# x^T of rows 512 to 2047: one transposing transfer for each block of 512 rows in place of five

## The chip, the cores and the metric

The kernel runs on one core of one Trainium2 chip. The metric is the device time of one execution in microseconds (us). Before the change the median of three runs is 182.51 us (182.13 to 182.59).

## The reference

Two linear-attention blocks A and B run over the same x (2048 rows, 640 columns, bf16), and a gate computed from x mixes their outputs row by row. For each block, with 32 heads of width 20:

```python
qkv = (x @ wqkv).reshape(B, S, 3, H, Dh)          # q, k, v by head
phi = lambda t: jnp.where(t > 0, t + 1, jnp.exp(t)) + 1e-6
pq, pk = phi(q), phi(k)
kv = jnp.einsum("bhsd,bhse->bhde", pk, v)
z = jnp.einsum("bhsd->bhd", pk)
num = jnp.einsum("bhqd,bhde->bhqe", pq, kv)
den = jnp.einsum("bhqd,bhd->bhq", pq, z)[..., None] + 1e-6
o = num / den                                     # then back to (S, D), @ wo
g = _sigmoid((x * gate_w).sum(-1, keepdims=True))
return g * a + (1 - g) * b                        # a, b: the two blocks' outputs
```

## The kernel before

Every projection on TensorE (PE) needs x with its 640 columns on the partitions, so the kernel holds a tile `xT` of 128 partitions x 5 x 2048: for each of the five groups c of 128 columns (a "column block"), the 2048 rows of x along the free axis. The rows are counted in blocks n of 512 (`HB`) and in chunks i of 128; block 1 is chunks 4 to 7, block 2 chunks 8 to 11, block 3 chunks 12 to 15.

Block 0 is not transposed by a transfer: its rows are loaded as they stand into `xn` and turned by PE (line 293), with VectorE (DVE) copying the result into `xT` (line 296). Blocks 1 to 3 come into `xT` straight from memory by transposing transfers, issued by SyncE (SP) at line 220: for each block five of them, one for each column block, 15 in all. The weights of k and q of block A are `wkA` and `wqA`; they are loaded from lines 203 and 217 ahead of the transposing transfers, on the same SP queue. Behind the transposing transfers SP issues the rows of blocks 1 to 3 once more, untransposed, into `xn` (line 1317), then v's weights `wvA` (1235) and the output weights `woA` (1242, 1245). All of SP's transfers are issued in the order of the code; each raises one of eight semaphores in turn (`DMAHW0` to `DMAHW7` in the listings below), and a transfer waits for the one that had the same semaphore before it.

The order on PE, DVE and ScalarE (ACT) is written out by hand in the string `FIRST`: each name is one step, and each engine executes what the steps give it in that order. The ones that matter here:

- `D4` to `D15` are the k projection of chunk 4 to 15 (`KFirst`, matmuls in `k_mm`, line 338). `D4` is cut into its five column blocks, `D4.c0` to `D4.c4`, with other work set between them:

```python
U0.n0 D2.top D4.c0 D4.c1 E.p1s E.P2 D4.c2 D4.c3 D3.clamp D3.lift0 tq3 sq03 U0.exp0 U0.lift0 tq1 D3.top D3.gl
sq01 D4.c4 E.exp0 tq2 D4.exp0 U0.n1 D4.gl sq02 ...
```

- `U0.n0` and `U0.n1` are a part of the q projection for block 0 and block 1 (line 393); `E.P1` and `E.P2` are q for block 0 alone (line 753).
- `sq03`, `sq01` and their like are sums and differences of two row blocks of `xT`, made by DVE (line 426) into `SQ` for the fast (Strassen-like) q product (line 527); `sq03` takes column blocks 0 and 1 of block 1, `sq01` column blocks 0 to 3.
- `D9` is the first step on block 2, `D15` the first on block 3.

Each reader of `xT` waits for the transfers that wrote what it reads. Where several readers on one engine follow one another, the first one carries the wait.

Of the kernel before, what the change touches and what calls it, by code (L numbers as in the profile page):

```python
# [9 lines left out]
P = 128  # L10
# [7 lines left out]
DT = D // P  # L18
# [3 lines left out]
HB = 512  # L22
# [56 lines left out]
def kernel(  # L79
# [11 lines left out]
    nc = tc.nc  # L91
    x2 = A_x.flatten_outer_dims()
# [43 lines left out]
    xT = persist.tile([P, DT, S], BF16, name="xT")  # L136
# [79 lines left out]
    for lo, hi in ((0, 2), (2, 4), (4, DT)):  # L216
        nc.sync.dma_start(out=wq[0][:, lo:hi, :], in_=wq_dram[0][:, lo:hi, 0:D])
    for n in range(1, NB):
        for c in range(DT):
            nc.sync.dma_start_transpose(  # L220
                out=xT[:, c, n * HB:(n + 1) * HB], in_=x2[n * HB:(n + 1) * HB, c * P:(c + 1) * P]
            )


    make_identity(nc, ident[:])
    for r in range(4):
# [3 lines left out]
        out=spread[:].rearrange("p (h t) -> p h t", t=TW), in_=I4[:, :, None].to_broadcast([P, H, TW])  # L230
    )
    for lo in range(0, HF, K6):
        part = maskE[:, lo:min(lo + K6, HF)]
        for sign, base in ((1, 0), (-1, Dh - 1)):
            nc.gpsimd.affine_select(
                out=part, in_=part, pattern=[[-sign * Dh, part.shape[1] // Dh], [0, Dh]],
# [3 lines left out]
    for rows, n in ((slice(0, 2 * H), H // 2), (slice(2 * H, P), H)):  # L240
        nc.gpsimd.tensor_copy(
            out=E4_rows[rows, 0:n], in_=I4[rows, 0:n, None].to_broadcast([rows.stop - rows.start, n, Dh])
# [1071 lines left out]
    with tc.manual_schedule():  # L1314
        pts = k_first()
        for n in range(1, NB):
            nc.sync.dma_start(
                out=xn[:, n * CB:(n + 1) * CB, :], in_=x2[n * HB:(n + 1) * HB, :].rearrange("(q p) d -> p q d", p=P)
# [325 lines left out]
```

## Time and profile before

| what | value |
|---|---|
| median of three runs | 182.51 us |
| the profiled execution's own time | 182.31 us |
| its span, from the first to the last instruction | 180.5 us |
| PE weight loads busy | 117.6 us |
| transposing transfers | 15, all on SP's queue |

The profile gives the busy time of each engine, a chain of waits followed back from the last instruction, the waits of each engine by releaser, and a timeline whose rows merge neighbouring instructions of one kind. "PEld" is PE's weight load, which runs beside the matmuls. For a transfer the trace has its time on the issuing queue ("SPq") and the time from the start of its issue to its landing, when the last of its data is there and its semaphore is complete. A busy PE is not PE at its peak, since the ends of matmuls are modelled.

### The profile page before, as it was taken

The page shows a single profiled execution, that of the slowest core. Times are in us where ns is not written, and L with a number is a line of the kernel's source. Part 1 is how long each engine was busy: PE and PEld are TensorE (multiplying, and loading weights), DVE is VectorE, ACT ScalarE, POOL GpSimd, SP SyncE. Part 2 cuts the span into 40 slices and gives each one's busy share as a digit, 9 for nine tenths or more (in the row PEclk, how much of TensorE's full clock was granted, in tenths as well). Part 3 has the DMA queues.
Part 4 walks back from the last instruction along what each step waited for, and adds up shares of the span by engine and source line. Part 5 has one row for each costly group of instructions (what it writes and reads, how often), then busy time and mean ns, then how long its engine had stood idle before and what let it go on. Part 6 is the DMA issues. An engine that isn't in the chain of part 4 may idle for free.

```text
span 180.5 us, 3397 instructions
## 1 busy us (share of the span) xinstructions
PE 176.9 (98%) x1276; PEld 117.6 (65%) x1276; DVE 152.0 (84%) x287; ACT 112.0 (62%) x235; POOL 4.4 (2%) x19
## 2 busy tenths in 40 slices
PE   8999999999999999999999999999999999999993
PEld 3666666665666677666656676766678777777772
DVE  1479999999999996888899997987988988686774
ACT  2098988999763434587778686774815756456410
POOL 7100000000000000000000000000000000000000
PEclk9999999999999999999999999999999999999999
DMA  5995449976035015000000024144901560133123
GB/s 184 284 187 91 97 106 291 356 158 182 0 112 185 8 54 181 2 0 0 2 4 2 0 32 153 31 127 123 264 3 48 167 153 0 40 137 119 73 101 120
DMA packets 21602, 18.85 MB, mean 104 GB/s; under 512 B 9298, under 2 KB 21074, under 8 KB 21586
## 3 DMA queue, kind: packets, MB, share of 16 engines
q1 hardware_dynamic: 20722, 17.82, 35.3%
q10 hardware_dynamic: 864, 0.82, 1.3%
q8 instruction: 10, 0.16, 0.4%
q14 instruction: 6, 0.05, 0.1%
HBM read 11.86 MB, written 4.80 MB: 92 GB/s over the span
## 4 chain that ended last, share of the span: by engine, by line
PE 96%; ACT 2%; DVE 1%; issue 0%
PE q L527 16%; PE kA L338 11%; PE kB L338 9%; PE gs L845 9%; PE gs L1333 9%; PE oy L1129 6%; PE oz L1129 5%; PE ox L1129 5%; PE ow L1129 4%; PE kB L527 3%; PE qA L393 3%; PE gB L815 2%; PE gA L815 2%; PE warm L252 2%; ACT e L551 1%; PE q L393 1%
## 5 line engine op out<-in xcount | busy, mean ns | idle before, releaser
L338 PEld LDWEIGHTS <-xT 128*128 128x128 bf16 x280 | 27.3, 98 | 15.1 <-DVE xT L296 0.2
L338 PE MATMUL kA<-wkA,xT 128*128 128x320 bf16 (+1 forms) x160 | 24.8, 304 | 0.0
L551 ACT ACTIVATE e<-q 128x512 bf16<-128x512 f32 x32 | 18.5, 599 | 5.7 <-PE q L527 5.2
L557 DVE TENSOR_SCALAR e<-e 128x640 bf16<-128x640 bf16 (+2 forms) x59 | 19.0, 334 | 2.9 <-ACT e L551 2.6
L338 PE MATMUL kB<-wkB,xT 128*128 128x320 bf16 x120 | 19.2, 299 | 0.0
L551 ACT ACTIVATE e<-kB 128x640 bf16<-128x640 f32 (+1 forms) x18 | 11.4, 647 | 7.3 <-PE kB L527 3.2
L551 ACT ACTIVATE e<-kA 128x640 bf16<-128x640 f32 x16 | 11.4, 720 | 5.8 <-PE kA L338 5.2
L533 DVE TENSOR_TENSOR q<-q,p 128x512 f32<-128x512 f32 x16 | 11.1, 695 | 1.7 <-PE q L527 1.2
L564 DVE SCALAR_TENSOR_TENSOR pk<-kB,e 128x640 bf16<-128x640 f32 (+1 forms) x16 | 11.6, 735 | 0.4
L1129 PEld LDWEIGHTS <-xT 128*128 128x128 bf16 x85 | 8.1, 98 | 2.9
L1129 PEld LDWEIGHTS <-pqTA 128*128 128x128 bf16 x85 | 8.1, 98 | 2.8
L1192 ACT COPY u<-ox 128x320 f32<-128x320 f32 x8 | 3.4, 425 | 10.4 <-PE ox L1129 10.4
L1129 PEld LDWEIGHTS <-pqTB 128*128 128x128 bf16 x80 | 7.8, 98 | 3.0
L527 PE MATMUL q<-xT,wqB 128*128 128x512 bf16 x32 | 9.7, 379 | 0.0
L1134 DVE TENSOR_TENSOR osb<-oz,u 128x320 bf16<-128x320 f32 (+2 forms) x18 | 7.9, 452 | 1.9 <-PE oz L1129 1.6
L527 PE MATMUL q<-SQ,TM 128*128 128x512 bf16 x32 | 8.5, 379 | 0.0
L1333 PEld LDWEIGHTS <-xn 128*128 128x128 bf16 x64 | 6.1, 98 | 3.1 <-issue 0.7
L815 PEld LDWEIGHTS <-xn 128*128 128x128 bf16 x64 | 6.3, 98 | 2.8
L845 PEld LDWEIGHTS <-xn 128*128 128x128 bf16 x64 | 6.1, 98 | 2.9 <-issue 0.7
L564 DVE SCALAR_TENSOR_TENSOR pk<-kA,e 128x640 bf16<-128x640 f32 x8 | 6.5, 818 | 0.4 <-DVE e L557 0.2
L564 DVE SCALAR_TENSOR_TENSOR pqTB<-q,e 128x512 bf16<-128x512 f32 x10 | 6.7, 682 | 0.0
L1129 PE MATMUL oz<-MB,xT 128*128 128x320 bf16 (+2 forms) x45 | 6.8, 284 | 0.0
(205 smaller groups left out, 376.3 us busy)
## 6 DMA issues: line engine op xcount, KB each, us to landing
out_dram<-osb SPq DMA_DIRECT2D x14, 160.0 KB, 1.8
xn<-in_A_x_dram SPq DMA_DIRECT2D x3, 640.0 KB, 5.8
wvA<-in_A_wqkv_dram SPq DMA_DIRECT2D x1, 800.0 KB, 9.1
wkB<-in_B_wqkv_dram SPq DMA_DIRECT2D x1, 800.0 KB, 4.5
wqB<-in_B_wqkv_dram SPq DMA_DIRECT2D x1, 800.0 KB, 7.1
wvB<-in_B_wqkv_dram SPq DMA_DIRECT2D x1, 800.0 KB
MA<-m_rows SPq DMA_DIRECT2D x1, 800.0 KB, 5.1
MB<-m_rows SPq DMA_DIRECT2D x2, 400.0 KB, 4.1
```

The costliest lines, as they stand in the source:

```text
L338: nc.tensor.matmul(pt[:, hf, 0:n], lhsT=xT[:, c, i * P:(i + 1) * P], rhs=wk[b][:, c, hf * HF:hf * HF + n], start=(c == 0), stop=(c == DT - 1),
L393: nc.tensor.matmul(dst, lhsT=mixed(wq[b][:, c, :], m), rhs=xT[:, c, n * HB:(n + 1) * HB], start=first, stop=last,)
L527: nc.tensor.matmul(dst, lhsT=left(c), rhs=right(c), start=first and k == 0, stop=last and k == len(cs) - 1, skip_group_check=not first,)
L533: nc.vector.tensor_tensor(out=dst, in0=acc, in1=sb, op=ALU.add)
L551: nc.scalar.activation(out=self.part(self.e, k), in_=self.srcs[k](), func=ACT.Exp)
L557: nc.vector.tensor_scalar(self.e, self.e, 1.0, EPS, op0=ALU.min, op1=ALU.add)
L564: nc.vector.scalar_tensor_tensor(out=self.part(self.dst, k), in0=src(), scalar=1.0 + EPS, in1=self.part(self.e, k), op0=ALU.add, op1=ALU.max,)
L815: nc.tensor.matmul(pt[:, hf, 0:HF], lhsT=xn[:, i, c * P:(c + 1) * P], rhs=pk[:, i, hf * HF:(hf + 1) * HF], start=(i == 0), stop=(i == ST - 1),
L845: nc.tensor.matmul(pt[:, n, 0:HF], lhsT=left[:, i, n * P:(n + 1) * P], rhs=right[:, i, :], start=(first and i == 0), stop=(i == hc - 1), s ...
L1129: nc.tensor.matmul(dst, lhsT=left[:, c, r0:r0 + P], rhs=right[:, c, :], start=(first and c == 0), stop=(c == DT - 1), skip_group_check=not ...
L1134: nc.vector.tensor_tensor(out=dst, in0=acc, in1=sb, op=ALU.add)
L1333: nc.tensor.matmul(dst[n], lhsT=left[:, i, n * P:(n + 1) * P], rhs=right[:, i, :], start=(first and i == 0), stop=(i == hc - 1), skip_grou ...
```

## The change

The five transfers of a block become one, which takes 512 rows with all 640 columns and writes 128 partitions x 5 x 512:

```diff
     for n in range(1, NB):
-        for c in range(DT):
-            nc.sync.dma_start_transpose(
-                out=xT[:, c, n * HB:(n + 1) * HB], in_=x2[n * HB:(n + 1) * HB, c * P:(c + 1) * P]
-            )
+        nc.sync.dma_start_transpose(out=xT[:, :, n * HB:(n + 1) * HB], in_=x2[n * HB:(n + 1) * HB, :])
```

Three lines less stand in the file, so later line numbers fall by 3. Nothing else is written differently.

SP's queue from the last of `wqA` to the first of the row loads, before (the names in brackets are what the issue waits for; seven of the 15 transposing transfers are shown, the first five and the last two):

```order
L217 DMA wqA_117<-in_A_wqkv_dram 128x640 [waits DMAHW3_49]
L220 DMA_TRANSPOSE xT_70<-in_A_x_dram 128x512 [waits DMAHW4_49]
L220 DMA_TRANSPOSE xT_70<-in_A_x_dram 128x512 [waits DMAHW5_49]
L220 DMA_TRANSPOSE xT_70<-in_A_x_dram 128x512 [waits DMAHW6_49]
L220 DMA_TRANSPOSE xT_70<-in_A_x_dram 128x512 [waits DMAHW7_49]
L220 DMA_TRANSPOSE xT_70<-in_A_x_dram 128x512 [waits DMAHW0_49]
...
L220 DMA_TRANSPOSE xT_70<-in_A_x_dram 128x512 [waits DMAHW1_49]
L220 DMA_TRANSPOSE xT_70<-in_A_x_dram 128x512 [waits DMAHW2_49]
L1317 DMA xn_71<-in_A_x_dram 128x4x640 [waits DMAHW3_49]
```

and with the change:

```order
L217 DMA wqA_117<-in_A_wqkv_dram 128x640 [waits DMAHW3_49]
L219 DMA_TRANSPOSE xT_70<-in_A_x_dram 128x5x512 [waits DMAHW4_49]
L219 DMA_TRANSPOSE xT_70<-in_A_x_dram 128x5x512 [waits DMAHW5_49]
L219 DMA_TRANSPOSE xT_70<-in_A_x_dram 128x5x512 [waits DMAHW6_49]
L1314 DMA xn_71<-in_A_x_dram 128x4x640 [waits DMAHW7_49]
```

The first transposing transfer stands at the same place behind the same wait; twelve transfers are gone between it and the row loads.

PE at `D4.c0` and `D4.c1`, before: the last weight load of `U0.n0` and the weight loads and matmuls of chunk 4.

```order
L393 LDWEIGHTS wqA_117 [waits DMAHW3_49]
L393 MATMUL qA_276<-xT_70,wqA_117 128x512
L338 LDWEIGHTS xT_70 [waits PE_49,DMAHW4_49]
L338 MATMUL kA_283<-wkA_106,xT_70 128x320 [waits Activation_49]
L338 LDWEIGHTS xT_70
L338 MATMUL kA_283<-wkA_106,xT_70 128x321
L338 LDWEIGHTS xT_70 [waits DMAHW5_49]
L338 MATMUL kA_283<-wkA_106,xT_70 128x320
```

and with the change:

```order
L390 LDWEIGHTS wqA_117 [waits DMAHW3_49]
L390 MATMUL qA_264<-xT_70,wqA_117 128x512
L335 LDWEIGHTS xT_70 [waits PE_49,DMAHW4_49]
L335 MATMUL kA_271<-wkA_106,xT_70 128x320 [waits Activation_49]
L335 LDWEIGHTS xT_70
L335 MATMUL kA_271<-wkA_106,xT_70 128x321
L335 LDWEIGHTS xT_70
L335 MATMUL kA_271<-wkA_106,xT_70 128x320
```

No instruction of PE moves. Before, `DMAHW4` and `DMAHW5` were the transfers of the first and second column block; now `DMAHW4` is the transfer of all five, and the later waits of chunk 4 (`D4.c1` to `D4.c4`) are gone.

## The prediction

> **What bounds the kernel now.** I began with the page: busy times, then the chain that ended last.
>
> ```profile
> span 180.5 us, 3397 instructions
> PE 176.9 (98%) x1276; PEld 117.6 (65%) x1276; DVE 152.0 (84%) x287; ACT 112.0 (62%) x235; POOL 4.4 (2%) x19
> PE 96%; ACT 2%; DVE 1%; issue 0%
> ```
>
> PE is busy for 176.9 of 180.5 us, and 96% of the chain is PE's. So all idle time of PE together is 3.6 us, and a change that only brings data earlier can win no more than its share of that. A change that brings data later costs whatever PE then waits. The next view is busy time by stretches, around the place where PE first needs the transposed rows (columns: stretch, its length, then PE, PEld, DVE, ACT, POOL busy with counts, granted clock, DMA share, GB/s).
>
> ```profile
> 6.40:12.00 5.60, 5.60 (x48) 4.11 (x46) 2.84 (x9) 2.62 (x8) 0.00 (x0) 1.00 1.21 245
> 12.00:13.00 1.00, 0.99 (x6) 0.35 (x4) 1.00 (x3) 0.96 (x3) 0.00 (x0) 1.00 0.77 167
> 13.00:30.00 17.00, 17.00 (x108) 10.63 (x107) 16.60 (x34) 14.82 (x32) 0.00 (x0) 1.00 0.56 124
> ```
>
> Between 6.4 and 30 us, in which all 15 transposing transfers are issued and land, PE loses 0.01 us by this view. The one gap is in the second stretch, and the timeline shows what it waits for: DVE's output of a k chunk, not a transfer.
>
> ```profile
> 12.67 0.80 PEld L393 LDWEIGHTS <-wqA 128*128 128x128 bf16 x5 [0.48 <-DVE pk L564]
> ```
>
> Last, the table of waits (columns: waited in us, times, longest). Only two of its rows name a transfer; one is the first row load at the start, the other a load of the late stage. None names `xT`.
>
> ```profile
> PEld L293 <- DMA xn<-in_A_x_dram: 0.5, 1, 0.5
> DVE TM L1065 <- DMA MB<-m_rows: 0.6, 1, 0.6
> ```
>
> So the 15 transfers are all hidden now. The question is whether three larger ones still are, above all the first.
>
> **The change part by part.** First what is removed: issue time on SP's queue.
>
> ```profile
> 4.25 1.49 SPq L217 DMA_DIRECT2D wqA<-in_A_wqkv_dram  x3
> 5.80 20.19 SPq L220 DMA_TRANSPOSE xT<-in_A_x_dram  x15
> 26.04 2.32 SPq L1317 DMA_DIRECT2D xn<-in_A_x_dram  x3
> ```
>
> 15 issues take 20.19 us, 1.35 each. SP waits for nobody there and nobody waits for SP's time itself, so its removal gives 0 directly. Behind it the row loads into `xn` start earlier: at the earliest after three issues of about 1.3 us, 5.8 + 3.9 = 9.7 instead of 26.0. Their first reader comes at 35.87 us.
>
> ```profile
> 35.87 0.68 DVE L1065 TENSOR_TENSOR S<-xn 128x1024 bf16<-128x1024 bf16 x1
> ```
>
> That reader does not wait now, so earlier rows give 0 too. What hides it is DVE's own work, busy 16.60 of 17 us up to 30. The earlier loads could disturb something: they bring the traffic of 28 to 38 us forward to where PE works on the same matmuls. But in the stretch with that traffic today PE loses nothing at three times the rate of the stretch before, so I take 0 for that as well.
>
> ```profile
> 28.00:30.00 2.00, 2.00 (x15) 1.18 (x13) 1.87 (x5) 1.82 (x5) 0.00 (x0) 1.00 0.96 330
> 30.00:32.00 2.00, 2.00 (x14) 1.25 (x12) 1.92 (x5) 1.39 (x4) 0.00 (x0) 1.00 1.05 369
> ```
>
> What is added is one wait: `D4.c0` on PE waited for the first fifth of block 1, and now waits for the whole block. It needs:
>
> ```profile
> 13.57 0.59 PEld L338 LDWEIGHTS <-xT 128*128 128x128 bf16 x4
> 13.79 0.71 PE L338 MATMUL kA<-wkA,xT 128*128 128x320 bf16 x4
> 13.84 0.67 DVE L426 TENSOR_TENSOR SQ<-xT 128x1024 bf16<-128x1024 bf16 x1
> ```
>
> The weight load starts at 13.57, takes 98 ns (the page's row of L338 weight loads, 27.3 us over 280), and its matmul starts at 13.79. It may slip to 13.7 before PE loses anything. Behind it on PE stands everything, since PE works in order; DVE's `sq03` at 13.84 waits for the same transfer and falls due a little later. So the cost is the landing of block 1 minus 13.7, or nothing. When does it land? These are the rows of single transfers (start of issue at the end of the first row, time to landing in the second): numbers 1, 3, 5 and 15.
>
> ```profile
> L338 PEld LDWEIGHTS <-xT 128*128 128x128 bf16 x280 | 27.3, 98 | 15.1 <-DVE xT L296 0.2
> ...
> L220 SPq DMA_TRANSPOSE xT<-in_A_x_dram x1: 1223/1223/1223, 5.8 to 5.8; - x1
> DMA to landing us min/median/max: 5.8/5.8/5.8
> ...
> L220 SPq DMA_TRANSPOSE xT<-in_A_x_dram x1: 1349/1349/1349, 8.4 to 8.4; - x1
> DMA to landing us min/median/max: 4.2/4.2/4.2
> ...
> L220 SPq DMA_TRANSPOSE xT<-in_A_x_dram x1: 1267/1267/1267, 11.1 to 11.1; - x1
> DMA to landing us min/median/max: 3.5/3.5/3.5
> ...
> L220 SPq DMA_TRANSPOSE xT<-in_A_x_dram x1: 1258/1258/1258, 24.7 to 24.7; - x1
> DMA to landing us min/median/max: 2.8/2.8/2.8
> ```
>
> Number 1 lands at 5.8 + 5.8 = 11.6, number 3 at 8.4 + 4.2 = 12.6, number 5 at 11.1 + 3.5 = 14.6, number 15 at 24.7 + 2.8 = 27.5. The last needs 2.8 us with nothing ahead of it; the first needed twice that. It queued behind weights: the second load of `wqA` was issued at 4.8 and landed at 10.6.
>
> ```profile
> L217 SPq DMA_DIRECT2D wqA<-in_A_wqkv_dram x1: 467/467/467, 4.8 to 4.8; - x1
> DMA to landing us min/median/max: 5.8/5.8/5.8
> ```
>
> So from number 1 to number 3 a backlog drains, two fifths in 1.0 us: 0.5 us for 131,072 B (512 x 128 x 2), or 262 GB/s. After that the transfers come at the pace of issue, not of data. The whole block, if its pieces are there to be drained, lands at 11.6 + 4 x 0.5 = **13.6 us**; stall 0. If the large transfer is issued piece by piece at today's pace, its last fifth starts at 5.8 + 4 x 1.26 = 10.8 and lands 2.8 to 3.5 us later, the times of numbers 15 and 5: 13.6 to 14.3. And number 5 itself, which carries the last piece of the block today, lands at 14.6. I take 14.6 as the upper end of this case, a stall of 14.6 - 13.7 = 0.9, and 0 as the lower, with no gain below it, because PE has no gap here that `xT` could close. Between them I take 13.8, a stall of **0.1 us**: the draining rows are the nearest, since the backlog is there in both kernels, and one issue replaces five.
>
> On signalling, the row comes first: today each fifth has its own landing, at 11.6, 12.6 and 14.6 for the ones shown. The Trainium skill, DMA: Bandwidth & Descriptors, section "Anatomy of one DMA", says that the semaphore update cannot fire until the last byte is confirmed in the target memory. That speaks against the change: by it the first fifth is worth nothing to PE until the fifth one has landed, which is the wait above. On rate, behind the 262 GB/s: the same page, section "Latency and other measured facts", gives a transposing transfer 261 GB/s where the middle dimension is not contiguous and 350 to 400 GB/s where it is; an estimate from that page's faster figure would be 655,360 B / 375 GB/s = 1.7 us for the block in place of 2.5, and the sum would stay the same, with a stall of 0.
>
> Blocks 2 and 3 have cover to spare. Their first readers on PE come at 22.74 and 29.21.
>
> ```profile
> 22.74 0.10 PEld L338 LDWEIGHTS <-xT 128*128 128x128 bf16 x1
> 29.21 0.10 PEld L338 LDWEIGHTS <-xT 128*128 128x128 bf16 x1
> ```
>
> At today's pace, 6.3 us of issue for each block, they would land near 20 and 27 (10.8 + 6.3 + 2.8 and 6.3 more); at the draining pace, near 16 and 19. Cost 0; without that cover it would be what they exceed these times by.
>
> The sum, against the profiled execution: 182.31 (180.5 of span and 1.8 around it) + 0 + 0 + 0.1 = 182.4. That execution was 0.2 us under the median of the three runs, 182.51; on the scale of the medians I forecast **182.6 us**.
>
> **The rivals.** What this kernel can tell from no change is about 0.3%, 0.55 us, so the forecast is "within".
>
> Rival 1, slower: the transfer's pieces are all generated before the first one moves. Then the issue lasts 5 x 1.26 = 6.3 us, to 12.1; the first fifth lands 2.8 - 1.26 = 1.5 us after that, the rest in 4 x 0.5 = 2.0: 15.6. The stall at `D4.c0` is 15.6 - 13.7 = 1.9 us, and PE, with 3.6 us of idle time in all, has no later gap to get it back: 184.5. For it speaks that each issue holds SP for 1.26 us, some 2.5 times what its data take to drain. Against it, a plain load of two and a half times the data (two column blocks of `wqA`, 327,680 B, above) holds the queue only 0.47 us, so a hold need not grow with the data. It decides from a landing of 13.7 + 0.55 = 14.25 on. Blocks 2 and 3 would land at 21.9 and 28.2, still in time.
>
> Rival 2, slower and milder: the block lands where its last fifth lands today, 14.6, because other traffic and not the issue delayed number 5. Stall 0.9: 183.4. Against it, number 5 stood only 3.5 us from its issue.
>
> Rival 3, faster: SP's queue is free up to 16 us earlier, and something behind it gains. It needs a reader that waits for `xn`, `wvA` or `woA` today, and the table of waits has none. The idle 0.48 us of the weight load at 12.67, behind DVE, is the only gap nearby; all of it would give 182.51 - 0.48 = 182.0, still inside the band. To reach 181.9 the change would have to shorten PE's work itself. The Trainium skill, DMA: Bandwidth & Descriptors, section "Bandwidth", has the rule to batch transfers to 1 MiB or more; it would make the transfers better, and by the rows above no earlier end comes of it.
>
> Rival 4: the change does not do what it says, and the large transfer is split again into fifths as it is issued. Then 182.5, which the forecast includes.
>
> **How the numbers follow.** Forecast with rival 4, a stall of 0 to 0.5 us: 0.63. Rival 1: 0.15. Rival 2: 0.15. Rival 3, or an unseen gain over 0.55 us: 0.07. So faster 0.07, same 0.63, slower 0.30. The forecast's own range is 182.2 to 183.0 (stall 0 to 0.5 with the scatter of the runs, 182.13 to 182.59). The range for 8 in 10 takes in rival 2: 182.1 to 183.7; rival 1 and most of rival 3 are left out.
>
> **What would show it.** In the profile of the changed kernel: three transposing issues; the first lands between 13 and 14.6; the weight loads of line 335 for chunk 4 start at 13.6 to 13.8 and the stretch 13 to 30 stays full; the row loads into `xn` are issued before 20 us; the wait table names no `xT` transfer, or one of a tenth. The prediction is wrong if PE waits for `xT` by over half a microsecond, at chunk 4, 8 or 12, or if the span moves with no PE wait at all.

## The result, and the profile after

The changed kernel takes 184.07 us (median of four runs, 183.88 to 184.24). The kernel before takes 182.32 us in four runs (182.13 to 182.59). The ratio is 1.0099 with a 95% interval of 1.0082 to 1.0116: slower by 1.75 us. The forecast was 182.6 us with a range up to 183.7, so the time lies above the range. The profiled execution took 183.96 us, beside 182.31 before.

The first lines of the page of the kernel after, and the engines' shares of its chain:

```profile
span 182.2 us, 3380 instructions
PE 176.5 (97%) x1276; PEld 116.9 (64%) x1276; DVE 152.1 (84%) x287; ACT 112.1 (62%) x235; POOL 4.4 (2%) x19
PE 81%; DVE 8%; DMA 7%; issue 2%; SPq 1%; DVEq 0%
```

PE is busy with the same 1276 matmuls for as long as before (176.5 us, before 176.9), and the span is 1.7 us longer. So what was lost is idle time of PE, or time after its last matmul. The chain, 96% PE before, now passes through a transfer (DMA 7%) and through DVE. The wait table of the kernel after for 10 to 20 us (waited in us, times, longest) names the transfer:

```profile
PEld L335 <- DMA xT<-in_A_x_dram: 1.8, 1, 1.8
DVE SQ L423 <- DMA xT<-in_A_x_dram: 1.4, 1, 1.4
```

One wait on each engine. The timeline of the kernel after shows the place: `U0.n0` (line 390), then `D4.c0` (line 335).

```profile
12.15 1.27 PE L390 MATMUL qA<-xT,wqA 128*128 128x512 bf16 x5
...
14.76 0.69 DVE L423 TENSOR_TENSOR SQ<-xT 128x1024 bf16<-128x1024 bf16 x1 [1.35 <-DMA xT<-in_A_x_dram]
14.77 0.39 PEld L335 LDWEIGHTS <-xT 128*128 128x128 bf16 x4 [1.83 <-DMA xT<-in_A_x_dram]
14.78 0.72 PE L335 MATMUL kA<-wkA,xT 128*128 128x320 bf16 x4 [1.35 <-ACT pqTA L551]
```

The matmul row names ACT, because an output of ACT happened to end last (in the kernel before this matmul starts at 13.79, ahead of that output, which starts at 14.68 there); its weight load, 0.01 us ahead of it, and DVE's `sq03`, which needs nothing of ACT, both name block 1. To see what PE lost, compare the distance from the start of `U0.n0` to the start of `D4.c0`. Before:

```profile
12.68 1.27 PE L393 MATMUL qA<-xT,wqA 128*128 128x512 bf16 x5
13.79 0.44 PE L338 MATMUL kA<-wkA,xT 128*128 128x320 bf16 x2
```

It was 1.11 us and is 2.63 us: 1.52 us lost. The landing behind it, from the rows of the first transposing transfer and of the last two loads of `wqA` after the change:

```profile
L217 SPq DMA_DIRECT2D wqA<-in_A_wqkv_dram x2: 468/474/479, 4.9 to 5.4; - x2
DMA to landing us min/median/max: 6.2/6.2/6.2
...
L219 SPq DMA_TRANSPOSE xT<-in_A_x_dram x1: 5847/5847/5847, 5.9 to 5.9; - x1
DMA to landing us min/median/max: 8.8/8.8/8.8
```

The weights land at 5.4 + 6.2 = 11.6, block 1 at 5.9 + 8.8 = 14.7 us, where the forecast had 13.8.

This is most of the loss, not all of it. `U0.n0` started 0.53 us earlier than before (12.15 against 12.68), `D4.c0` 0.99 us later. Twenty microseconds on, at chunk 15 (`D15`), the difference grows once more. The last lines ahead of it on DVE and its matmuls on PE, before:

```profile
28.12 0.32 DVE L557 TENSOR_SCALAR e<-e 128x640 bf16<-128x640 bf16 x1
28.57 0.82 DVE L564 SCALAR_TENSOR_TENSOR pk<-kA,e 128x640 bf16<-128x640 f32 x1
...
29.44 1.52 PE L338 MATMUL kA<-wkA,xT 128*128 128x320 bf16 x10
```

and after:

```profile
28.86 0.60 ACT L776 COPY q<-R 128x512 f32<-128x512 f32 x1
29.09 0.32 DVE L554 TENSOR_SCALAR e<-e 128x640 bf16<-128x640 bf16 x1
29.96 0.82 DVE L561 SCALAR_TENSOR_TENSOR pk<-kA,e 128x640 bf16<-128x640 f32 x1 [0.55 <-ACT q L776]
...
30.84 1.52 PE L335 MATMUL kA<-wkA,xT 128*128 128x320 bf16 x10 [0.28 <-DVE pk L561]
```

From the start of the one DVE instruction to the next it was 0.45 us and is 0.87: DVE is held 0.42 us with the same work on both sides. The row puts it down to ACT's `q`, but that had ended at 28.86 + 0.60 = 29.46, half a microsecond ahead, so the trace shows nothing that DVE still waited for. PE, which needs this output (the "top" of a k chunk) for its next buffer, then starts `D15` 30.84 - 29.44 = 1.40 us late, 0.41 more than at `D4.c0`. From there to the last output transfer the difference stays: 178.07 us on SP's queue before, 179.46 after, 1.39. The span ends 1.7 us later, so a third piece of 0.3 us lies behind the last transfer. Before:

```profile
178.07 0.33 SPq L1149 DMA_DIRECT2D out_dram<-osb  x1
```

and after:

```profile
179.46 0.33 SPq L1146 DMA_DIRECT2D out_dram<-osb  x1
```

Both land 1.6 us later, at 179.7 and 181.1; the spans end at 180.5 and 182.2, so 0.8 us and 1.1 us after it.

The account of the 1.7 us by which the two profiled spans differ is then: -0.5 at the start, +1.5 at `D4.c0`, +0.4 at `D15`, +0.3 at the end. The first is no doing of the change: in the kernels below `U0.n0` starts at 11.9 to 13.0 us, with block 1 whole or in five.

### The profile page after: what moved, and what is told of

Same layout as the page of the kernel before. It is cut to its first block, busy times and chain, and to the rows that moved or that the text cites. A ratio compares the mean times of both kernels' runs of the same rounds, so it can differ in the third digit from the quotient of the medians.

```text
span 182.2 us, 3380 instructions
## 1 busy us (share of the span) xinstructions
PE 176.5 (97%) x1276; PEld 116.9 (64%) x1276; DVE 152.1 (84%) x287; ACT 112.1 (62%) x235; POOL 4.4 (2%) x19
## 4 chain that ended last, share of the span: by engine, by line
PE 81%; DVE 8%; DMA 7%; issue 2%; SPq 1%; DVEq 0%
PE q L524 14%; PE kB L335 9%; PE gs L842 9%; PE gs L1330 8%; PE oy L1126 6%; DMA xT<-in_A_x_dram 5%; PE oz L1126 5%; PE ox L1126 4%; PE ow L1126 4%; PE kA L335 4%; PE kB L524 3%; PE gB L812 2%; PE gA L812 2%; DMA xn<-in_A_x_dram 2%; DVE pk L561 1%
## 5 line engine op out<-in xcount | busy, mean ns | idle before, releaser
L335 PE MATMUL kA<-wkA,xT 128*128 128x320 bf16 (+1 forms) x160 | 24.2, 299 | 1.6 <-ACT pqTA L551 1.4
L530 DVE TENSOR_TENSOR q<-q,p 128x512 f32<-128x512 f32 x16 | 11.1, 696 | 1.7 <-PE q L524 1.2
L561 DVE SCALAR_TENSOR_TENSOR pk<-kB,e 128x640 bf16<-128x640 f32 (+1 forms) x16 | 11.6, 735 | 0.4
```

The source lines that it names most:

```text
L335: nc.tensor.matmul(pt[:, hf, 0:n], lhsT=xT[:, c, i * P:(i + 1) * P], rhs=wk[b][:, c, hf * HF:hf * HF + n], start=(c == 0), stop=(c == DT - 1),
L530: nc.vector.tensor_tensor(out=dst, in0=acc, in1=sb, op=ALU.add)
L561: nc.vector.scalar_tensor_tensor(out=self.part(self.dst, k), in0=src(), scalar=1.0 + EPS, in1=self.part(self.e, k), op0=ALU.add, op1=ALU.max,)
```

## The experiments

Each kernel was timed beside the kernel before on the same chip, the last two once, the others several times. Ratios are to the kernel before, with 95% intervals.

**Which block.** Block 1 in five, blocks 2 and 3 whole:

```diff
     for n in range(1, NB):
-        nc.sync.dma_start_transpose(out=xT[:, :, n * HB:(n + 1) * HB], in_=x2[n * HB:(n + 1) * HB, :])
+        groups = [(c, c + 1) for c in range(DT)] if n == 1 else [(0, DT)]
+        for lo, hi in groups:
+            dst = xT[:, lo:hi, n * HB:(n + 1) * HB] if hi - lo > 1 else xT[:, lo, n * HB:(n + 1) * HB]
+            nc.sync.dma_start_transpose(out=dst, in_=x2[n * HB:(n + 1) * HB, lo * P:hi * P])
```

> Block 1 again in five transfers, blocks 2 and 3 in one each. In the profile of the change PE loses 1.52 us at D4.c0 (the landing of block 1, 14.73 us) and 0.45 us at 30.8 us, where DVE starts one instruction half a microsecond late and ACT stands 1 us with no releaser shown. Theory W (the loss is the wait for the whole of block 1): the first stall is gone, PE runs through at D4.c0, and the time is that of the kernel before, 182.3 us, ratio 1.000 +- 0.003. Theory L (part of the loss comes from the row and weight loads that are issued 7 us earlier and run beside DVE's and ACT's instruction fetches): those loads are early here too (near 19 us), so 0.4 to 0.5 us of the loss stays, 182.7 to 182.8, with the stall near 30 us in the profile.

Measured: 182.14 us, ratio 1.0000 (0.9986 to 1.0013). SP's queue in this kernel:

```profile
19.44 1.68 SPq L1317 DMA_DIRECT2D xn<-in_A_x_dram  x3
```

The row loads start at 19.4 us instead of 26.0, and neither they nor the two whole blocks cost or win anything. Then the other half, block 1 whole and blocks 2 and 3 in five:

```diff
-        groups = [(c, c + 1) for c in range(DT)] if n == 1 else [(0, DT)]
+        groups = [(c, c + 1) for c in range(DT)] if n > 1 else [(0, DT)]
```

> Block 1 in one transfer, blocks 2 and 3 in five each, so that the loads behind them are issued near 24.5 us, almost as late as before. Theory W: the stall of 1.0 to 1.5 us at D4.c0 stays and the one near 30 us is incidental; 183.3 to 184.0 us. Theory L: the stall near 30 us is gone, and the time is 0.4 us under that of the change (184.07), 183.6 us. If the late landing of block 1 came from the large transfer that follows it, block 1 lands here near 13.4 us (its packets end at 13.3 in the change's trace), the stall is about 0.2 us and the time 182.5.

Measured: 183.11 us, ratio 1.0059 (1.0038 to 1.0081). The profiled execution, at 184.25 us the slowest of its nine, waits for `xT` as the changed kernel does:

```profile
PEld L338 <- DMA xT<-in_A_x_dram: 1.6, 1, 1.6
PE kA L338 <- DMA xT<-in_A_x_dram: 1.2, 1, 1.2
DVE SQ L426 <- DMA xT<-in_A_x_dram: 1.1, 1, 1.1
DVE pk L564 <- ACT q L779: 0.5, 1, 0.5
```

So with block 1 in five the change loses nothing, and the hold of DVE at `D15` (the last row; it names ACT here too) comes with block 1 whole, though nothing of blocks 2 and 3 was changed here. By the medians this kernel loses 1.0 us, not 1.75: what stands behind it on the queue counts too (below).

**Is the wait at `D4.c0` the whole of it?** The reader moved back, behind other work that was there:

```diff
-U0.n0 D2.top D4.c0 D4.c1 E.p1s E.P2 D4.c2 D4.c3 D3.clamp D3.lift0 tq3 sq03 U0.exp0 U0.lift0 tq1 D3.top D3.gl
+U0.n0 D2.top E.p1s E.P2 D4.c0 D4.c1 D4.c2 D4.c3 D3.clamp D3.lift0 tq3 sq03 U0.exp0 U0.lift0 tq1 D3.top D3.gl
```

> The change, with E.p1s and E.P2 (six matmuls on block 0, 1.29 us on PE) moved ahead of D4.c0 in the written order. Theory W: the wait at D4.c0 is covered for 1.29 us of its 1.52, PE stalls 0.2 us or not at all, and the time falls by 1.0 to 1.3 to 182.8 to 183.1. If the loss were not PE's wait for block 1, the time would stay at 184.0.

Measured: 183.7 us (182.98 to 184.69 in six runs), ratio 1.0104 (1.0078 to 1.0131). A miss: the time did not fall. The profiled execution is the fastest of the six, and in it PE has no wait at `D4.c0`, while it loses something at 21.1 us, for ACT, and at `D15` as before:

```profile
21.09 1.54 PE L335 MATMUL kA<-wkA,xT 128*128 128x320 bf16 x10 [0.21 <-ACT pk L551]
...
29.80 1.52 PE L335 MATMUL kA<-wkA,xT 128*128 128x320 bf16 x10 [0.28 <-DVE pk L561]
```

So the new order hides the wait and brings one of its own. Why its other runs are up to 1.7 us slower than this one isn't known; one profile doesn't tell.

**What stands behind block 1 on the queue.** The row loads of each block moved up behind its transposing transfer, so that a plain load follows block 1 and not another transposing transfer:

```diff
     for n in range(1, NB):
         nc.sync.dma_start_transpose(out=xT[:, :, n * HB:(n + 1) * HB], in_=x2[n * HB:(n + 1) * HB, :])
+        nc.sync.dma_start(
+            out=xn[:, n * CB:(n + 1) * CB, :], in_=x2[n * HB:(n + 1) * HB, :].rearrange("(q p) d -> p q d", p=P)
+        )
...
-        for n in range(1, NB):
-            nc.sync.dma_start(
-                out=xn[:, n * CB:(n + 1) * CB, :], in_=x2[n * HB:(n + 1) * HB, :].rearrange("(q p) d -> p q d", p=P)
-            )
```

> The change, with each row load into xn issued right behind the transposing transfer of its block, so that a plain load and not the next transposing transfer follows block 1. If the next large transposing transfer delays the completion of the one before it: block 1 lands near 13.4 us in place of 14.7, the stall at D4.c0 is 0 to 0.3 us and the time 182.4 to 182.9. If the late landing is block 1's own (its pieces wait for the slowest of the weight loads, then 2.5 us of data): it lands at 14.5 to 15 as in the change, and the time stays near 184.

Measured: 183.0 us, ratio 1.0048 (1.003 to 1.0065). The rows of its first transposing transfer and, below them, its timeline: block 1 lands at 6.0 + 7.8 = 13.8 us, and PE loses nothing (12.74 to 13.86 is 1.12 us); the 0.30 us that the weight load waited ran beside the matmuls of `U0.n0`.

```profile
L219 SPq DMA_TRANSPOSE xT<-in_A_x_dram x1: 5659/5659/5659, 6.0 to 6.0; - x1
DMA to landing us min/median/max: 7.8/7.8/7.8
```

```profile
12.74 1.28 PE L393 MATMUL qA<-xT,wqA 128*128 128x512 bf16 x5
...
13.84 0.39 PEld L338 LDWEIGHTS <-xT 128*128 128x128 bf16 x4 [0.30 <-DMA xT<-in_A_x_dram]
13.86 0.71 PE L338 MATMUL kA<-wkA,xT 128*128 128x320 bf16 x4
```

So without a wait of PE at `D4.c0` 0.9 us of the loss are still there, and the hold at `D15` is one part of it.

**The hold of DVE.** In kernels with block 1 whole, DVE has two wait instructions fewer ahead of that top, since it waits for one transfer instead of five. Counted in the trace, waits included, the held top is DVE's 64th instruction in every kernel so far that shows the hold, and the 66th where there is none. So the count alone was changed: the changed kernel with two idle memsets more, and the kernel before with two memsets fewer (they go to GpSimd):

```diff
     nc.vector.memset(tiny[:], LOGS * EPS)
+    pad = persist.tile([P, 2], FP32, name="pad")
+    for k in range(2):
+        nc.vector.memset(pad[:, k:k + 1], 0.0)
```

> The change with two small extra memsets of 128x1 at the start of DVE's queue, where DVE has idle time until 4.4 us. In every kernel so far that loads block 1 in one transfer, the 64th instruction of DVE in the trace, a top of a k chunk, starts 0.46 us after the one before it with all its waits met, and PE loses 0.42 to 0.44 us at D15 for it; in the kernel before and in the one with block 1 in five that top is the 66th and starts after 0.04 us, since DVE has two waits more ahead of it. Theory P (the loss belongs to a place in DVE's instruction stream): with two more instructions ahead, the top is the 66th again, its gap is 0.04 us, PE's loss at D15 is gone, and the time falls by 0.42 to 183.3 (183.7 less 0.4; the wait for block 1 varies by half a microsecond from run to run). Theory L (loads beside instruction fetches): nothing changes, the 0.46 us gap stays at that top. The stall at D4.c0 stays in both.

```diff
-    nc.vector.memset(ones[:], 1.0)
-    nc.vector.memset(lift[:], 1.0 + EPS)
...
+    nc.gpsimd.memset(ones[:], 1.0)
+    nc.gpsimd.memset(lift[:], 1.0 + EPS)
```

> The kernel before, with two of DVE's memsets at the start given to GpSimd, behind its own start work, so that DVE's queue is two instructions shorter ahead of the same top. Nothing of the transfers changes. Theory P: the top of D8 or D15 that was the 66th is now the 64th, starts 0.46 us late, PE loses 0.42 us there, and the time is 182.1 + 0.4 = 182.5, ratio 1.0023. Theory L: same as the kernel before, 182.1.

Measured: the change with two more 183.03 us, ratio 1.0069 (1.0046 to 1.0092); the kernel before with two fewer 182.54 us, ratio 1.0027 (1.0011 to 1.0043). DVE in the change with two more:

```profile
28.55 0.32 DVE L557 TENSOR_SCALAR e<-e 128x640 bf16<-128x640 bf16 x1
29.00 0.82 DVE L564 SCALAR_TENSOR_TENSOR pk<-kA,e 128x640 bf16<-128x640 f32 x1
```

and DVE and PE in the kernel before with two fewer:

```profile
28.30 0.82 DVE L564 SCALAR_TENSOR_TENSOR pk<-kA,e 128x640 bf16<-128x640 f32 x1 [0.55 <-ACT q L779]
...
29.18 1.52 PE L338 MATMUL kA<-wkA,xT 128*128 128x320 bf16 x10 [0.28 <-DVE pk L564]
```

The hold went in the one (0.45 us from start to start) and came in the other, which has all fifteen transposing transfers of the kernel before. It hangs on the place in DVE's stream, not on the transfers.

**The end of the program.** SP waits there for the eight semaphores of its transfers in a fixed order, in five wait instructions that start 0.06 to 0.07 us apart by the trace of the changed kernel. Twelve transfers fewer move the last output transfer to another of the eight, which is waited for in the first of the five instead of the fifth: four more steps behind the last landing, 0.25 us. To test that alone, the kernel before with four more transfers:

```diff
         for n in range(1, NB):
-            nc.sync.dma_start(
-                out=xn[:, n * CB:(n + 1) * CB, :], in_=x2[n * HB:(n + 1) * HB, :].rearrange("(q p) d -> p q d", p=P)
-            )
+            rows = x2[n * HB:(n + 1) * HB, :].rearrange("(q p) d -> p q d", p=P)
+            for lo, hi in ((0, CB),) if n == 1 else ((0, 1), (1, 2), (2, CB)):
+                nc.sync.dma_start(out=xn[:, n * CB + lo:n * CB + hi, :], in_=rows[:, lo:hi, :])
```

> The kernel before, with the row loads of blocks 2 and 3 into xn cut into three each, four transfers more. That moves the semaphore of every later transfer on by four of the eight, as the change's twelve fewer do. At the end SP waits for the eight transfer semaphores in a fixed order, one after the other, about 0.065 us each. In the change the transfer that lands last carries the first semaphore waited for, in the kernel before the last one; the time from the last landing to the end of the span is 1.09 us against 0.84. Theory E (the end costs 0.25 us by the turn of the semaphores): the same 1.09 us here, time 182.1 + 0.25 = 182.35, ratio 1.0014. If the difference at the end has another cause in the change: 0.84 us and 182.1.

Measured: 182.36 us, ratio 1.0020 (1.0006 to 1.0034). In its timeline the last output transfer is issued at 178.43; it lands 1.6 us later, at 180.0, and the span ends at 181.1, which is the 1.1 us of the changed kernel. The twelve traces agree: the span ends 1.09 to 1.10 us after the last landing in the eight kernels in which that transfer carries the semaphore of the first wait, and 0.84 us in the four in which it carries that of the fifth. It is the count that decides, not block 1: e1 issues eight transfers fewer, a full turn of the eight semaphores, and has 0.84; e2 issues four fewer and has 1.10. The row of f3's last output transfer:

```profile
178.43 0.33 SPq L1149 DMA_DIRECT2D out_dram<-osb  x1
```

**All three undone with block 1 still whole:** the row loads between (removed further down, as in e4), the split of f3 in them, and the two memsets (the last as in f1). The part of the edit that is new:

```diff
         nc.sync.dma_start_transpose(out=xT[:, :, n * HB:(n + 1) * HB], in_=x2[n * HB:(n + 1) * HB, :])
+        rows = x2[n * HB:(n + 1) * HB, :].rearrange("(q p) d -> p q d", p=P)
+        for lo, hi in ((0, CB),) if n == 1 else ((0, 1), (1, 2), (2, CB)):
+            nc.sync.dma_start(out=xn[:, n * CB + lo:n * CB + hi, :], in_=rows[:, lo:hi, :])
```

> Blocks in one transfer each, with all three suspected costs taken away at once: each row load right behind its block's transposing transfer (block 1 then landed at 13.8 us in place of 14.7), two more memsets on DVE, and the row loads of blocks 2 and 3 cut into three, which turns the semaphores back. If the three costs are all there is, the time is that of the kernel before, 182.1 to 182.4, with no PE loss over 0.1 us after 13 us and 0.84 us from the last landing to the end. If something else of the change costs time, it stays above 182.6.

Measured: 182.25 us, ratio 1.0014 (1.0000 to 1.0027): of 1.75 us lost by the change, 0.1 (by the medians) to 0.3 (by the ratio) are left. The profiled execution, at 182.82 us the slowest of its twelve, still waits: by the rows of its first transposing transfer block 1 lands at 5.9 + 8.4 = 14.3, and by the timeline below them PE loses 14.31 - 12.86 - 1.11 = 0.34 us at `D4.c0`, more than the 0.1 us expected; the row of the matmul now names the transfer:

```profile
L222 SPq DMA_TRANSPOSE xT<-in_A_x_dram x1: 6288/6288/6288, 5.9 to 5.9; - x1
DMA to landing us min/median/max: 8.4/8.4/8.4
```

```profile
12.86 1.28 PE L396 MATMUL qA<-xT,wqA 128*128 128x512 bf16 x5
...
14.31 0.72 PE L341 MATMUL kA<-wkA,xT 128*128 128x320 bf16 x4 [0.17 <-DMA xT<-in_A_x_dram]
```

**One place or several?** The changed kernel with one memset more, and with four, where f1 has two:

```diff
+    for k in range(1):
+        nc.vector.memset(pad[:, k:k + 1], 0.0)
```

> The change with one more memset of one column on DVE at the start, so that the top before D15 is the 65th DVE instruction of the trace instead of the 64th. If the hold belongs to the 64th place alone, the top starts 0.04 us behind its wait instruction and PE loses nothing before D15 near 29 to 31 us. If the hold covers a stretch of places, of which f1 at the 66th has just left the end, it is still there: the top starts 0.46 us late and PE loses 0.42 us. The wait for block 1 is untouched in both: 0.2 to 1.5 us at D4.c0, by when block 1 lands (13.8 to 14.8). Span 181.0 to 182.2 without the hold, 181.4 to 182.6 with it.

```diff
+    for k in range(4):
+        nc.vector.memset(pad[:, k:k + 1], 0.0)
```

> The change with four more memsets on DVE at the start: the top before D15 is the 68th DVE instruction. If the hold belongs to one place near the 64th, it stays away as with two memsets, and PE loses nothing before D15. If it comes back at intervals of four places, or if it belongs to the top and came and went with something else, the top starts 0.46 us late again and PE loses 0.42 us. The wait for block 1 as in the other kernel: 0.2 to 1.5 us.

Measured, one time each: 183.35 and 183.82 us, beside 181.91 for the kernel before. The top is the 65th and the 68th instruction, and not held in either: from start to start 29.35 - 28.89 = 0.46 and 29.77 - 29.32 = 0.45 us. PE lost 14.58 - 12.76 - 1.11 = 0.71 us at `D4.c0` with one and 15.01 - 12.60 - 1.11 = 1.30 with four. So of the places 64, 65, 66 and 68 only the 64th is held.

It isn't the only such place, though. In f1 another top, a wait instruction just ahead of it, stands at the 192nd place of DVE's stream, three times 64:

```profile
88.96 0.33 DVE L557 TENSOR_SCALAR e<-e 128x640 bf16<-128x640 bf16 x1
89.77 0.82 DVE L564 SCALAR_TENSOR_TENSOR pk<-kB,e 128x640 bf16<-128x640 f32 x1 [0.48 <-DVE e L557]
```

From start to start it is 0.81 us; in e1 and f4, where the same top is the 193rd, 0.44 and 0.43. PE loses nothing by it there. The 256th instruction stands behind a wait in five kernels (e1, e2, f2, f3, f4) and is not held (0.05 us). What the held places have in common is not shown.

**The landings side by side.** Worked out from the trace's semaphore records: each transfer raises its semaphore sixteen times, and has landed with the last. The column "first" is the time from the last landing of `wqA` to block 1's first record, "all" to its last.

| kernel | behind block 1 | wqA landed | first | all | block 1 landed | PE lost |
|---|---|---|---|---|---|---|
| the change | transposing, whole block | 11.56 | 2.12 | 3.17 | 14.73 | 1.52 |
| e3 | the same | 10.55 | 2.18 | 3.21 | 13.76 | (other order) |
| f1 | the same | 10.93 | 2.18 | 3.26 | 14.19 | 0.29 |
| g1 | the same | 11.17 | 2.17 | 3.36 | 14.53 | 0.71 |
| g4 | the same | 11.58 | 2.12 | 3.38 | 14.96 | 1.30 |
| e2 | transposing, a fifth | 12.25 | 2.09 | 2.77 | 15.02 | 1.34 |
| e4 | plain load | 11.49 | 2.14 | 2.31 | 13.80 | 0.01 |
| f4 | plain load | 11.97 | 2.13 | 2.29 | 14.26 | 0.34 |

In all eight the first record comes 2.1 to 2.2 us after the weights. With a plain load behind, all sixteen come within 0.17 us; with another whole block behind, they are spread over 1.0 to 1.3 us (f1: nine by 13.24, seven from 14.03 to 14.19). PE needs the last one. The Trainium skill, DMA: Bandwidth & Descriptors, section "Why a DMA increments its semaphore by 16 and not by 1", says that a transfer runs on up to sixteen engines that finish independently and that only the full count means all data landed; the records spread over a microsecond agree with it. It doesn't say why some should be late.

The traces also record each packet that the DMA engines move, and these show on which side of the landing the difference lies. Block 1 is 2,560 packets of 256 B, and 32 of 4 B end it. The last of them ends at 13.35 us in the changed kernel and at 13.30 in e4, 1.8 us behind the weights in both, and 1.8 to 1.9 us in the other six. So up to there the transfer behind makes no difference. Only the records behind the last packet differ: the last comes 0.5 us later in e4 and f4, 1.0 in e2, and 1.4 to 1.6 in the five with a whole block behind. Why isn't shown, and "a plain load behind it" is no rule that holds for every block: block 2 of e4 and f4 has one too, and its last record comes 1.5 us after the other fifteen.

## Why the prediction was wrong

**What bounds the kernel: right.** PE sets the start of the last output transfer: what is lost at `D4.c0` and `D15`, 1.0 + 0.4 us, is found again there (1.39).

**Issue time removed, 0; earlier row loads, 0; blocks 2 and 3 covered, 0: right.** e1 has all three and ratio 1.0000. The issue of a whole block was taken as 1.3 us in the estimate of the row loads ("5.8 + 3.9 = 9.7") and lasted 5.8, 3.3 and 3.6 us; it costs nothing either. The landing of block 3 "near 27" is 26.2 by the prediction's own sum (10.8 + 6.3 + 2.8 + 6.3); it was 20.7, and the term stays 0.

**The added wait: mechanism right, size wrong, 1.5 us for 0.1.** The step that failed is "Between them I take 13.8, a stall of 0.1 us: the draining rows are the nearest". The draining itself was well estimated: five fifths of 0.5 us are 2.5 us behind the weights, and where a plain load follows, the block needs 2.3. But the estimate took the transfer alone; another whole block stands behind it, and then the last records come 3.2 to 3.4 us after the weights, 0.9 to 1.1 us more. The table shows this: e4 and f4 against the first five kernels. By the packets block 1 was drained at 13.35 us; with the 0.5 us to its last record that e4 shows it would have landed at 13.85, the forecast's 13.8, but that step took 1.4. The weights too landed half a microsecond later (11.6) than the 11.1 from which the first fifth drained before; they vary between 10.6 and 12.3 with block 1 whole and between 11.1 and 11.7 in the four kernels with it in five, and why stays open. And the need was not fixed at 13.7: PE came to `D4.c0` 0.5 us earlier in this execution, which made the wait longer by what it had won, so that the net loss there was 1.0 us.

**Two terms were missing.** The sum took the effect on DVE's stream and on the end of the program as 0 without a word. Measured 0.42 us (f1 takes it away, f2 brings it to the kernel before: 0.4 us of its median) and 0.25 us (f3: 0.22 of the median). Net 1.0, 0.4 and 0.25 make 1.65 us, the difference of the two profiled executions (1.75 by the medians).

**Rival 1** (184.5, all pieces generated before the first moves) is nearest in time and was not what happened: by the packets of the changed kernel, block 1's first piece moves at 9.05 us, and some 900 of its 2,560 have started by 11.7, where the issue ends. That the hold of 6.3 us on the queue was about right (5.8) was luck: in the eight kernels with block 1 whole it lasted 4.9 to 6.5 us and ended 0.2 to 0.3 us after the weights had landed, so it went with them and not with five times 1.26 us. By the rival the block lands 1.5 + 2.0 = 3.5 us after the end of its issue. In e4 the issue ended at 6.0 + 5.7 = 11.7 and the block landed 2.1 us later; in f4 at 12.2, also 2.1; in the changed kernel it was 3.0 us, of which the late records are 0.9. **Rival 2** (14.6, "because other traffic and not the issue delayed number 5") had the landing, 14.7, and very nearly the cause: number 5 in the kernel before shows the two groups as well, twelve records by 14.07 and four from 14.47 to 14.56. What it called "other traffic" it did not name, so the landing was right with the cause left open. The 3.5 us from its issue, held against it, say nothing of what is behind it. **Rivals 3 and 4** fell: nothing got faster, and SP issues three transfers.

## What to carry to other kernels

Where a consumer waits for pieces, one large transfer in place of five takes the early pieces away and has landed only with the last of its sixteen records; read the landing off a trace in which the same neighbours stand on the queue, since here the transfer behind it was worth 0.9 us. In a kernel whose bounding engine has no slack, price what an edit does to the other engines' streams and to the count of transfers too: 0.4 and 0.25 us came from two wait instructions and twelve transfers fewer. Only block 1 needed its pieces; blocks 2 and 3 can be whole at no cost (e1), and no version here beats the kernel before.

## What the runs showed of the hardware that was not expected

- DVE's 64th instruction started 0.46 us after its last wait instruction ended in the five kernels in which it is a top behind one (0.04 to 0.05 us at the 65th, 66th and 68th place), and f1's 192nd 0.42 us after. Theories that tied it to the loads beside it fell: it is there in e2 with late row loads and absent in e1 with early ones. That it is the loading of instructions is not shown: the traces record the transfers that carry instructions, and in the five kernels none of them runs between 19.3 and 31.4 us, while the holds lie between 27.8 and 30.3. The Trainium skill, Runtime: NRT & Kernel Launch, section "Instruction fetch mechanics", says that instructions are fetched in blocks of 256 and that crossing a block's border costs one step that is mostly hidden; the trace numbers only the instructions it records, so no run here tells whether the 64th of them stands at such a border.
- The end of the program took 0.84 or 1.09 to 1.10 us after the last landing, by which of eight semaphores the last transfer carried (four and eight kernels).
- In the changed kernel a whole transposing transfer held SP's queue for 5.8 us behind the weights, and 3.3 and 3.6 us after that. In the eight kernels with block 1 whole the first hold ended 0.2 to 0.3 us after the weights had landed.
- Between the last packet of block 1 and the last record of its semaphore lay 0.5 us in e4 and f4 and 1.4 to 1.6 us in the five kernels with another whole block behind it.
